# Weight conversions on VectorE and paced by step, the third pair of a Strassen-Winograd MLP in round one from its fifth chunk on, sums in PSUM, and mixing tiles in the tokens' places

## Chip, core and metric

One core of a Trainium2 chip runs the whole kernel. The metric is device microseconds of one execution. PE is TensorE, DVE is VectorE, ACT is ScalarE, POOL is GpSimd, and SP is the engine that issues all loads and stores here. All large products are made of three float32r products (high x high, high x low, low x high), so every operand stands as a high part and a low part (the rest that rounding leaves).

## The reference

Sizes: batch 8, 8 heads, 576 tokens, 512 channels, 2048 hidden channels; all weights arrive as float64.

```python
def phi(x):
    proj = np.einsum('bhsd,df->bhsf', x, w_phi)
    proj = proj - np.max(np.abs(proj), axis=-1, keepdims=True)
    return np.concatenate([np.exp(proj), np.exp(-proj)], axis=-1)
# attention: linear attention with phi(q), phi(k); num / den
# MLP: layer norm over 512 channels, then
    ch = np.maximum(xn @ w_ch1, 0.0) @ w_ch2
    x = x + ch
# mixing:
    theta = x @ w_theta
    y = (np.einsum('ts,bsd->btd', w_tok_r, x * cos(theta))
         + np.einsum('ts,bsd->btd', w_tok_i, x * sin(theta)))
    u = x + y
    out = u + np.maximum(u @ w_ch, 0.0)
```

## The kernel before

The time has four parts. **Attention** takes the first 600 us or so. The layer norm and the first quarter of the MLP (`mlp_a`, four of sixteen blocks of 128 hidden channels) run beside it in 18 chunks of 256 tokens and go on for its last six chunks after it; `tokens` in `mlp_a` transposes the normalised tokens on PE, ACT takes the high part from PSUM, DVE the low part, and the sum of both goes to DRAM as `xnd` for later.

**Pair rounds.** The other twelve hidden blocks are six pairs. A `Pair` holds the seven combinations of two 256 x 256 weight blocks that a Strassen-Winograd product needs (`wa`) and its part of the second weight (`wd`). Tokens go in nine chunks of 512; `tokens_b` loads a chunk (`xt`), forms four sums or differences, and splits seven operands (a11, a12, a22, s1 to s4) into high (ACT) and low (DVE). Round one runs pairs 0 to 2 over the nine chunks, round two pairs 3 to 5; a step is one pair on one chunk. In a step `Hidden.first` and `second` make the seven products in PSUM (tiles pa, of which there are two, pb and pc, one each), DVE adds what belongs together, ACT makes the relu's high part and DVE its low part. `flush_b` makes the down part of the step before (24 matmuls of 512 columns into four accumulators `acc`). Between rounds the sum of residual and output goes through DRAM (`xqd`).

**Conversion.** A float64 weight block comes in as 64-bit integers (`raw`, three places). ACT takes the magnitude, DVE makes three instructions of integer bits and one product (L110, L111, L112, L117), ACT writes the high part. Low parts (`lo_pool`, L66) and the four weight differences `tw` (L587 to L590) of the pairs are on POOL. A pair is six pieces of such work (`prep` yields six times). One piece is asked for after each step, at low priority; the scheduler that orders the instructions on each engine may place it earlier. Pairs 0 to 2 are converted before round one, pairs 3 to 5 in it, and the mixing's weights (26 pieces, `loads_mix`) in round two.

**Mixing.** For each batch: transposes of the tokens (`tp`), theta (`th`), its sine and cosine through ACT, DVE and POOL, the product over tokens (`mx`), and the channel product (`ch`).

Each engine works off its instructions in a fixed order, which the scheduler writes at build time. SP's queue is in order too.

## Time and profile before

| | us |
|---|---|
| three timed runs | 1777.98, 1778.2, 1774.35 (median 1777.98) |
| profiled execution | 1779.11, of which the span from first to last instruction is 1777.3 |
| PE busy | 1677.1 (94%) |
| DVE busy | 1286.8 (72%) |
| ACT busy | 805.4 (45%) |
| POOL busy | 781.8 (44%) |

The page counts an engine as busy from an instruction's start to its end; neighbouring instructions overlap a little, so a sum of durations is larger than the busy time. PE's granted clock is 1.00 where it runs at its upper level (2.4 GHz); a mean below that says that a part of a stretch ran at the lower one (1.2 GHz).

### The profile page before, as it was taken

To read this page: it belongs to the slowest core of one execution; us is meant where nothing else is said; L and a number is where in the kernel's file an instruction comes from. 1 tells how busy PE (TensorE), PEld (TensorE's weight loads), DVE (VectorE), ACT (ScalarE), POOL (GpSimd) and SP (SyncE) were. 2 spreads that over 40 slices of the span, in tenths; PEclk is the share of its full clock that TensorE was granted. 3 is DMA by queue.
4 is the path that set the end of the run, shared out by engine and by line. 5 is a ranking of instruction groups with operands and counts; after the bars stand their busy time and mean duration, and the time that the engine had idled before them with its cause. 6 is when DMAs were issued, how large, how long until landed. Compare 5 with 4: busy or idle time off the path is not lost.

```text
span 1777.3 us, 29747 instructions
## 1 busy us (share of the span) xinstructions
PE 1677.1 (94%) x11272; PEld 1524.4 (86%) x11272; DVE 1286.8 (72%) x2292; ACT 805.4 (45%) x1644; POOL 781.8 (44%) x684
## 2 busy tenths in 40 slices
PE   7899999899999888879999998999989999999999
PEld 5787998898899687768988887888978999999999
DVE  8988898888887696995555699555547656656662
ACT  6675666566666444543333354333333223322230
POOL 7786787687685376651111333121123222222220
PEclk9999999999999999999999999999999999999999
DMA  5333333233331454653231676331271211112101
GB/s 192 86 106 117 97 108 111 78 110 117 103 119 48 140 177 169 236 167 108 96 118 72 252 244 228 101 143 72 88 251 37 69 51 38 55 46 67 59 20 41
DMA packets 107966, 201.65 MB, mean 113 GB/s; under 512 B 8368, under 2 KB 58416, under 8 KB 104496
## 3 DMA queue, kind: packets, MB, share of 16 engines
q1 hardware_dynamic: 107824, 199.76, 34.1%
q8 instruction: 89, 1.46, 0.4%
q14 instruction: 53, 0.43, 0.1%
HBM read 125.73 MB, written 69.80 MB: 110 GB/s over the span
## 4 chain that ended last, share of the span: by engine, by line
PE 67%; DVE 20%; issue 4%; POOL 4%; ACT 3%; DMA 2%; SPq 0%; DVEq 0%; POOLq 0%; ACTq 0%
PE acc L77 5%; PE acc L75 5%; PE acc L76 5%; PE mx L75 4%; PE mx L76 4%; PE mx L77 4%; PE pa L76 2%; PE pa L77 2%; PE pa L75 2%; DVE bits L111 2%; PE ch L77 2%; PE ch L75 2%; PE ch L76 2%; DVE bits L112 2%; DVE hl L703 2%
## 5 line engine op out<-in xcount | busy, mean ns | idle before, releaser
L75 PE MATMUL acc<-wd,hh 128*128 128x512 f32 x432 | 173.5, 402 | 7.2 <-ACT hh L702 4.2
L77 PE MATMUL acc<-wd,hl 128*128 128x512 f32 x432 | 163.7, 401 | 16.2 <-DVE hl L703 16.2
L76 PE MATMUL acc<-wd,hh 128*128 128x512 f32 x432 | 172.6, 400 | 0.0
L633 POOL TENSOR_TENSOR s<-xt 128x512 f32<-128x512 f32 x18 | 26.3, 1462 | 310.4 <-DMA xt<-xnd 283.2
L75 PE MATMUL mx<-xs 128*128 128x288 f32 x512 | 151.1, 296 | 0.5 <-POOL xs L57 0.4
L76 PE MATMUL mx<-xs 128*128 128x288 f32 x512 | 151.2, 296 | 0.0
L77 PE MATMUL mx<-xs 128*128 128x288 f32 x512 | 149.4, 296 | 0.0
L273 DVE TENSOR_TENSOR ys<-pj,m 128x512 f32<-128x512 f32 (+1 forms) x160 | 99.6, 626 | 34.0 <-ACT pf L283 19.3
L703 DVE SCALAR_TENSOR_TENSOR hl<-c,hh 128x256 fp32r<-128x256 f32 x162 | 101.1, 630 | 22.6 <-ACT hh L702 22.4
L77 PEld LDWEIGHTS acc<-wd,hl 128*128 128x128 f32 x432 | 80.1, 189 | 38.9 <-DVE hl L703 22.1
L271 DVE TENSOR_REDUCE m<-pj 128x4 f32<-128x512 f32 (+1 forms) x160 | 98.6, 622 | 13.7 <-PE pj L77 13.1
L57 POOL TENSOR_SCALAR xs<-sc 128x512 fp32r<-128x512 f32 x72 | 47.5, 659 | 134.8 <-DVE sc L935 133.2
L702 ACT ACTIVATE hh<-c 128x256 fp32r<-128x256 f32 x162 | 66.4, 415 | 85.0 <-DVE c L696 82.7
L66 POOL TENSOR_TENSOR kpl<-pf,kph 128x512 fp32r<-128x512 f32 (+1 forms) x75 | 96.2, 1283 | 19.4 <-ACT kph L60 16.8
L75 PEld LDWEIGHTS acc<-wd,hh 128*128 128x128 f32 x432 | 82.9, 192 | 21.3 <-ACT hh L702 5.2
L283 ACT ACTIVATE pf<-ys 128x512 f32<-128x512 f32 (+1 forms) x160 | 85.5, 586 | 34.0 <-DVE ys L273 13.3
L66 POOL TENSOR_TENSOR qp<-pf,qp 128x512 fp32r<-128x512 f32 (+1 forms) x66 | 80.6, 1226 | 39.8 <-ACT qp L60 39.6
L75 PEld LDWEIGHTS mx<-xs 128*128 128x128 f32 x512 | 96.2, 188 | 1.4 <-POOL xs L57 1.2
L696 DVE TENSOR_TENSOR c<-pc,u 128x256 f32<-128x256 f32 x108 | 44.9, 416 | 71.9 <-ACT u L691 71.7
L76 PEld LDWEIGHTS mx<-xs 128*128 128x128 f32 x512 | 96.2, 188 | 0.0
L77 PEld LDWEIGHTS mx<-xs 128*128 128x128 f32 x512 | 95.6, 188 | 0.1
L76 PE MATMUL kv<-kpl,vh 128*65 128x256 f32 x300 | 87.9, 293 | 6.2 <-DVE kpl L63 6.0
(263 smaller groups left out, 6157.1 us busy)
## 6 DMA issues: line engine op xcount, KB each, us to landing
xt<-xnd SPq DMA_DIRECT2D x36, 512.0 KB, 4.7
raw<-in_w SPq DMA_DIRECT2D x32, 512.0 KB, 4.2
in<-in_va SPq DMA_DIRECT2D x30, 325.0 KB, 3.0
xd<-xo SPq DMA_DIRECT2D x48, 192.0 KB, 2.1
x<-xd SPq DMA_DIRECT2D x36, 256.0 KB, 2.9
xnd<-xt SPq DMA_DIRECT2D x18, 512.0 KB, 3.4
xpd<-x SPq DMA_DIRECT2D x36, 256.0 KB, 2.2
x<-xpd SPq DMA_DIRECT2D x18, 512.0 KB, 4.5
```

Of the source, the lines that this page charges most:

```text
L57: G.tensor_scalar(dst, src, scale, 0.0, op0=ALU.mult, op1=ALU.add)
L66: G.tensor_tensor(dst, src, f32(hi), op=ALU.subtract)
L75: T.matmul(out_, lhsT=lh, rhs=rh, start=start, stop=False, **kw)
L76: T.matmul(out_, lhsT=lh, rhs=rl, start=False, stop=False, **kw)
L77: T.matmul(out_, lhsT=ll, rhs=rh, start=False, stop=stop, **kw)
L111: V.scalar_tensor_tensor(bits, hi32, -(1 << 30), bits, op0=ALU.bitwise_and, op1=ALU.bitwise_or)
L271: V.tensor_reduce(m[:, :2 * n], pv, axis=AX.X, op=ALU.max, apply_absolute_value=True)
L273: V.tensor_tensor(ys[:, :2 * n, :], pv, m[:, :2 * n].unsqueeze(2).to_broadcast([P, 2 * n, NF]), op=ALU.subtract)
L283: A.activation(kp[:, :2 * n, s, :], ys[:, :2 * n, :], AF.Exp, scale=sc)
L696: V.tensor_tensor(c, ps, t, op=ALU.add)
L702: A.activation(h, c, AF.Relu)
L703: V.scalar_tensor_tensor(l, c, 0.0, f32(h), op0=ALU.max, op1=ALU.subtract)
```

## The change

Low parts and weight differences of the conversions go from POOL to DVE. Only pairs 0 and 1 are converted before round one; pair 2 is converted during the first four chunks, which have two steps each, and takes part from the fifth chunk on. Round two makes up for it: its first four chunks have four steps (pairs 2 to 5). `advance` sets how many pieces have been asked for after each step: 24 over the 22 steps of round one, and the 26 of the mixing from the fifth chunk of round two on. The first chunk's token sums are on DVE. The copy of the transposed tokens for DRAM, in chunks after the attention, is an ACT copy from PSUM in place of a POOL sum. DVE's sums for c11 and c12 are written back into pb and pc; c22 uses a place of `raw` until the conversions are over. The mixing's tiles take the places of the token tiles, its weights are loaded during the last chunk, and its first tiles are prepared ahead of the last down part.

```diff
@@ tokens, in mlp_a
-                G.tensor_tensor(xt[:, :, o], f32(xh[:, :, o]), f32(xl[:, :, o]), op=ALU.add)
+                if wide(ch):
+                    A.activation(xt[:, :, o], tp, AF.Copy)
+                else:
+                    G.tensor_tensor(xt[:, :, o], f32(xh[:, :, o]), f32(xl[:, :, o]), op=ALU.add)
@@ Pair.prep
-            G.tensor_tensor(t[:, 0], b12, b11, op=ALU.subtract)
+            V.tensor_tensor(t[:, 0], b12, b11, op=ALU.subtract)
...
-                lo(dl, x, dh)
+                lo_vec(dl, x, dh)
...
-    spare = Pair(NR + 1, NR)
-    slots = [Pair(m, m) for m in range(NR)]
-    gl = (None for q in slots for _ in q.prep(p_st))
+    early = [Pair(m, m) for m in range(2)]
+    gl = (None for q in early for _ in q.prep(p_st))
@@ tokens_b
-        G.tensor_tensor(s1, a21, a22, op=ALU.add)
-        G.tensor_tensor(s2, s1, a11, op=ALU.subtract)
-        G.tensor_tensor(s3, a11, a21, op=ALU.subtract)
-        G.tensor_tensor(s4, a12, s2, op=ALU.subtract)
+        eng.tensor_tensor(s1, a21, a22, op=ALU.add)
+        eng.tensor_tensor(s2, s1, a11, op=ALU.subtract)
...
+            if n == "s1":
+                eng.tensor_tensor(s3, a11, a21, op=ALU.subtract)
+                eng.tensor_tensor(s4, a12, s2, op=ALU.subtract)
...
-    cur = tokens_b(0)
+    cur = tokens_b(0, V)
@@ loads_mix (three places)
-            split64(p_st, wth[:, c, :], wths[c][:, 0, :], wths[c][:, 1, :], pool_lo=True)
+            split64(p_st, wth[:, c, :], wths[c][:, 0, :], wths[c][:, 1, :])
@@ Hidden
-            c11 = self.plus(b, p1, "c11")
-            self.relu(c11, 0, 0)
+            V.tensor_tensor(b, b, p1, op=ALU.add)
+            self.relu(b, 0, 0)
...
-            c22 = self.plus(c, u3, "c22")
-            self.relu(c22, 1, 1)
+            t = p_st.tile([P, NC_], F32, name="c22", tag="raw", bufs=RAWB) if pace else p_hb.tile([P, NC_], F32, name="c22")
+            V.tensor_tensor(t, c, u3, op=ALU.add)
+            self.relu(t, 1, 1)
...
-            c12 = self.plus(self.c, self.u2, "c12")
-            self.relu(c12, 0, 1)
+            V.tensor_tensor(self.c, self.c, self.u2, op=ALU.add)
+            self.relu(self.c, 0, 1)
@@ loads_b
+        prs[2] = Pair(2, 2)
+        yield from prs[2].prep(p_st)
+        for i in range(2):
+            q = Pair(4 + i, 3)
             yield from q.prep(p_st)
+            q.keep(wx_d[i])
+        prs[3] = Pair(3, 3)
+        yield from prs[3].prep(p_st)
@@ the rounds
+    LOADB, LOADX = 24, 26
+    def advance(r, to):
+        goal = (LOADB, LOADX)[r] * to
+        with tc.high_priority(offset=LOWP):
+            while steps[r] < goal:
+                next(gl if r == 0 else gx, None)
+                steps[r] += 1
...
+            ms = ([0, 1] + ([2] if ch >= LATE else [])) if r == 0 else (([2] if ch < LATE else []) + [3, 4, 5])
...
+                if r == 0:
+                    if ch < LATE:
+                        advance(0, done / (2 * LATE) * 6 / LOADB)
+                    else:
+                        advance(0, 6 / LOADB + (done - 2 * LATE) / (3 * (NQ - LATE) - 2) * (1 - 6 / LOADB))
+                elif ch >= LATE:
+                    advance(1, min(1, (done - 4 * LATE) / (3 * (NQ - LATE) - 4)))
@@ the mixing's start
     x4, pre = shared_prep(0)
     bs[0].start(x4)
+    early(0)
     shared(0, pre)
+    early(1)
+    bs[0].theta(0)
+    flush_b()
@@
+LATE = 4
```

Three places show how the engines' orders move. POOL in round one, from the token sums of its second chunk on (`s` is a token sum, `tw`, `wa` and `wd` are the pair's conversion); before:

```order
L633 TENSOR_TENSOR s_9675<-xt 128x512
L635 TENSOR_TENSOR s_9677<-xt 128x512
L634 TENSOR_TENSOR s_9676<-s_9675,xt 128x512
L636 TENSOR_TENSOR s_9678<-xt,s_9676 128x512
L587 TENSOR_TENSOR tw<-vs 128x256
L588 TENSOR_TENSOR tw<-vs 128x256
L589 TENSOR_TENSOR tw<-vs,tw 128x256
L66 TENSOR_TENSOR wa_8264<-vs,wa_8264 128x512
```

and now (the token sums are named `c`):

```order
L647 TENSOR_TENSOR c_9502<-xt 128x512
L652 TENSOR_TENSOR c_9504<-xt 128x512
L648 TENSOR_TENSOR c_9503<-c_9502,xt 128x512
L653 TENSOR_TENSOR c_9505<-xt,c_9503 128x512
L647 TENSOR_TENSOR c_9750<-xt 128x512
L652 TENSOR_TENSOR c_9752<-xt 128x512
```

Between one chunk's token sums and the next one's POOL has nothing left. DVE in round one, from a c11 sum on (of the fifth step before, `c<-pb`, and of the fourth now, `pb<-pb`); before:

```order
L696 TENSOR_TENSOR c_9846<-pb,p_9838 128x256
L110 TENSOR_SCALAR bits<-raw 128x512
L111 SCALAR_TENSOR_TENSOR bits<-raw,bits 128x512
L746 TENSOR_TENSOR x<-acc_9394,x 128x512
L696 TENSOR_TENSOR c_9769<-pc,u_9767 128x256
L746 TENSOR_TENSOR x<-acc_9395,x 128x512
L112 SCALAR_TENSOR_TENSOR bits<-raw,bits 128x512
L703 SCALAR_TENSOR_TENSOR hl<-c_9846,hh 128x256
L703 SCALAR_TENSOR_TENSOR hl<-c_9769,hh 128x256
L703 SCALAR_TENSOR_TENSOR hl<-pa,hh 128x256
L117 SCALAR_TENSOR_TENSOR val<-mag,bits 128x512
```

and now:

```order
L720 TENSOR_TENSOR pb<-pb,p_9669 128x256
L63 TENSOR_TENSOR wa<-vs,wa 128x512
L594 TENSOR_TENSOR tw<-vs,tw 128x256
L63 TENSOR_TENSOR wa<-vs,wa 128x256
L63 TENSOR_TENSOR a11l<-xt,a11h 128x512
L756 TENSOR_TENSOR xo<-acc_9328,xo 128x512
L756 TENSOR_TENSOR xo<-acc_9329,xo 128x512
L63 TENSOR_TENSOR a12l<-xt,a12h 128x512
L728 TENSOR_TENSOR c_9597<-pc,u_9595 128x256
L63 TENSOR_TENSOR wa<-tw,wa 128x512
L712 SCALAR_TENSOR_TENSOR hb<-pb,hb 128x256
```

The low parts of `wa` now stand in DVE's queue between the sums and the relus; the steps after this one hold no conversion. PE at the first transpose of the mixing (`tp`), inside the last down part (`acc`); before:

```order
L77 MATMUL acc_15405<-wd_12477,hl 128x512
L910 MATMUL tp<-ident,x 128x128 x4
L75 MATMUL acc_15402<-wd_12477,hh 128x512
L76 MATMUL acc_15402<-wd_12477,hh 128x512
L75 MATMUL acc_15403<-wd_12477,hh 128x512
L76 MATMUL acc_15403<-wd_12477,hh 128x512
L77 MATMUL acc_15402<-wd_12477,hl 128x512
L77 MATMUL acc_15403<-wd_12477,hl 128x512
L75 MATMUL th<-xs,xh 128x512
```

and now:

```order
L937 MATMUL tp<-ident,xs 128x128 x4
L77 MATMUL acc_15280<-wd,hb 128x512
L77 MATMUL acc_15281<-wd,hb 128x512
L75 MATMUL acc_15280<-wd,hb 128x512
L76 MATMUL acc_15280<-wd,hb 128x512
L77 MATMUL acc_15280<-wd,hb 128x512
L75 MATMUL acc_15281<-wd,hb 128x512
L76 MATMUL acc_15281<-wd,hb 128x512
L77 MATMUL acc_15281<-wd,hb 128x512
L75 MATMUL acc_15278<-wd,hb 128x512
L76 MATMUL acc_15278<-wd,hb 128x512
```

The transposes moved ahead by eight matmuls of the down part; four more of these follow the rows shown.

## Rows read from the trace of the kernel before

**Rows 1.** The page: busy time, share of the span and instructions of each engine.

```profile
span 1777.3 us, 29747 instructions
...
PE 1677.1 (94%) x11272; PEld 1524.4 (86%) x11272; DVE 1286.8 (72%) x2292; ACT 805.4 (45%) x1644; POOL 781.8 (44%) x684
```

**Rows 2.** Busy time by stretch: length, PE, weight loads, DVE, ACT, POOL, clock, DMA.

```profile
100.00:150.00 50.00, 49.66 (x379) 43.19 (x378) 43.77 (x94) 35.59 (x71) 39.25 (x34) 1.00 0.40 114
597.00:690.60 93.60, 83.04 (x496) 73.16 (x494) 80.15 (x123) 35.73 (x69) 57.23 (x42) 0.93 0.52 173
690.60:797.00 106.40, 84.56 (x474) 72.42 (x475) 97.79 (x136) 51.19 (x116) 61.40 (x46) 0.94 0.59 208
797.00:1000.00 203.00, 202.77 (x1262) 181.73 (x1261) 112.00 (x208) 74.62 (x180) 32.91 (x25) 1.00 0.34 121
1000.00:1110.00 110.00, 99.68 (x588) 86.50 (x586) 104.36 (x187) 53.53 (x131) 46.22 (x37) 0.97 0.68 229
1110.00:1174.00 64.00, 62.58 (x386) 55.58 (x387) 37.36 (x65) 23.14 (x57) 12.87 (x9) 1.00 0.35 120
1312.00:1360.00 48.00, 40.41 (x211) 32.73 (x210) 37.25 (x55) 21.12 (x36) 23.13 (x27) 0.96 0.34 106
```

**Rows 3.** Waits of PE from 690.6 to 797: us in total, times, longest.

```profile
PE acc L77 <- DVE hl L703: 11.2, 6, 3.2
```

**Rows 4.** DVE by groups, 690.6 to 797: busy us, mean ns, idle before.

```profile
L111 DVE SCALAR_TENSOR_TENSOR bits<-raw,bits 128x512 int32<-128x512 int32 x14 | 17.5, 1247 | 0.3
L703 DVE SCALAR_TENSOR_TENSOR hl<-c,hh 128x256 fp32r<-128x256 f32 x21 | 14.9, 721 | 1.0 <-ACT hh L702 1.0
L112 DVE SCALAR_TENSOR_TENSOR bits<-raw,bits 128x512 int32<-128x512 int32 x13 | 11.7, 901 | 0.1
L110 DVE TENSOR_SCALAR bits<-raw 128x512 int32<-128x512 int32 x14 | 11.3, 807 | 0.1
L117 DVE SCALAR_TENSOR_TENSOR val<-mag,bits 128x512 f32<-128x512 f32 x13 | 10.7, 823 | 0.1
...
L703 DVE SCALAR_TENSOR_TENSOR hl<-pa,hh 128x256 fp32r<-128x256 f32 x7 | 2.9, 411 | 0.0
```

**Rows 5.** DVE by groups, 797 to 1000.

```profile
L112 DVE SCALAR_TENSOR_TENSOR bits<-raw,bits 128x512 int32<-128x512 int32 x2 | 1.4, 685 | 0.0
L111 DVE SCALAR_TENSOR_TENSOR bits<-raw,bits 128x512 int32<-128x512 int32 x1 | 0.7, 693 | 0.0
L110 DVE TENSOR_SCALAR bits<-raw 128x512 int32<-128x512 int32 x1 | 0.4, 426 | 0.0
```

**Rows 6.** Timeline of DVE, 848 to 850.2: start, us.

```profile
848.41 0.68 DVE L63 TENSOR_TENSOR a22l<-xt,a22h 128x512 fp32r<-128x512 f32 x1
849.01 0.69 DVE L63 TENSOR_TENSOR s4l<-s,s4h 128x512 fp32r<-128x512 f32 x1
```

**Rows 7.** Timeline of DVE, 855 to 859.

```profile
855.96 1.37 DVE L703 SCALAR_TENSOR_TENSOR hl<-c,hh 128x256 fp32r<-128x256 f32 x1
857.25 0.41 DVE L696 TENSOR_TENSOR c<-pb,p 128x256 f32<-128x256 f32 x1
857.59 0.41 DVE L703 SCALAR_TENSOR_TENSOR hl<-pa,hh 128x256 fp32r<-128x256 f32 x1
```

**Rows 8.** Timeline of POOL, 855 to 859.

```profile
855.74 1.31 POOL L635 TENSOR_TENSOR s<-xt 128x512 f32<-128x512 f32 x1
857.00 1.48 POOL L634 TENSOR_TENSOR s<-s,xt 128x512 f32<-128x512 f32 x1
```

**Rows 9.** Waits of PE from 1312 to 1360.

```profile
PE th L75 <- ACT xh L60: 3.1, 3, 1.6
PE tp L910 <- DMA x<-x2d: 2.9, 1, 2.9
```

**Rows 10.** The page's DMA issues: KB each, median us from issue to landing.

```profile
xt<-xnd SPq DMA_DIRECT2D x36, 512.0 KB, 4.7
raw<-in_w SPq DMA_DIRECT2D x32, 512.0 KB, 4.2
```

More of the change, by code (lines that the diff above doesn't have):

```diff
@@ L731, in down @@
                     o = slice(i * P, (i + 1) * P)
[L732 to L733 removed]
+                    mm3(acc[i], self.hb[:, 0, j, o], self.hb[:, 1, j, o], self.q.wd[:, 0, j, :],
+                        self.q.wd[:, 1, j, :], start and j == 0, stop and j == 1)
     def flush_b():
[L736 to L739 removed]
+        hid, acc, r, ch, first, last = pend
+        hid.down(acc, first, last)
+        if last:
+            x = p_hb.tile([P, 2 * CT, DM], F32, name="xo")
             if r == 0:
@@ L819, in body @@
-    wtks = [t[:, i] for q in slots for t in [in_slot("wa", q.slot, [3, 2, S])] for i in range(3)]
-    wtk_t = wtks
-    wchs = [t[:, i] for q in slots[:2] for t in [in_slot("wd", q.slot, [2, 2, DM])] for i in range(2)]
-    wths = [(t[:, 0, :], t[:, 1, :]) for t in wths]
-    wtks = [(t[:, 0, :], t[:, 1, :]) for t in wtks]
+                pend = (hid, acc, r, ch, n == 0, n == len(ms) - 1)
+                if n == len(ms) - 1 and not (r and last):
+                    cur = tokens_b(0 if last else ch + 1, G)
@@ new lines, in body @@
+                done += 1
+                if r == 0:
[5 more added lines that the diff above has]
+                    advance(1, min(1, (done - 4 * LATE) / (3 * (NQ - LATE) - 4)))
+                if r and last:
+                    k = (3, 0, 1)[n]
+                    t = in_slot("wa", k, [3, 2, S])
+                    for i in range(3):
+                        wtks[MIXO[3 * n + i]] = t[:, i]
+                        SY.dma_start(out=f32(t[:, i]), in_=wtk_d[MIXO[3 * n + i]])
@@ L824, in body @@
+                if r == 0 and last and n >= 1:
+                    prs[3 + n] = Pair(3 + n, n - 1).back(wx_d[n - 1])
+            if r and ch == NQ - 2:
+                advance(1, 1)
+                s_st.close()
+                pace = False
+        if r == 0:
+            advance(0, 1)
+    s_ps.close()
     s_xm, pm = opened(name="xm", bufs=1, side="left")
+    s_ps = ExitStack()
+    ps_tr, ps_th = pool("xtp", 1), pool("xth", 2)
     class Slots:
@@ L1001, in body @@
     s_ps.close()
-    s_p1.close()
+    s_ac.close()
     s_xm.close()
-    s_xc.close()
+    s_hb.close()
+    s_xb.close()
     s_wb.close()
```

183 lines of the change are left out of this document (82 added, 101 removed).

## The prediction

> **What bounds the kernel now.** I read the page's shares first: PE is busy 94% of a span of 1777.3 us [rows 1]. The change alters no matmul: the order of the built programs holds 11174 PE instructions on both sides. So it can only give back time in which PE stands or runs slowly. The second view, busy time by stretch, shows where that is [rows 2]. From 797 to 1000 us PE is full: 1262 matmuls in 203 us, 6.217 per us, so a step of the pair rounds (66 matmuls by the code: 42 of the up part, 24 of the down part) takes 10.62 us. At that pace the 474 matmuls of 690.6 to 797 are 76 us of work in 106 us: 30 lost. The 588 of 1000 to 1110 are 94.6 in 110: 15 lost; 1110 to 1174 loses 2 more. Before round one (597 to 690.6) shapes differ, so I count idle time, 93.6 - 83.0 = 10.6, and the lower clock, 7% of 83 = 5.8: 16 lost. The start of the mixing (1312 to 1360) loses 7.6 + 4% of 40 = 9 likewise. In all 72 us; a change of this kind can't give back more.
>
> In the three stretches that hold conversions DVE is busy 86%, 92% and 95%; from 797 to 1000, where it is 55%, nothing is lost [rows 2]. The list of waits says whom PE waits for in round one: the down part for the low halves of the relu on DVE, 11.2 us in six waits [rows 3]. The groups of DVE say why these come late [rows 4, 5]: in the conversion stretch the first or of the bits (L111) takes 1247 ns against 693 in the quiet stretch, the shift (L110) 807 against 426, and the relu that reads its sum from SBUF (L703, hl<-c) 721, while the same relu that reads PSUM (hl<-pa) stays at 411. The timeline shows the partner: a relu of 1.37 us [rows 7] lies on POOL's subtraction of 1.31 us that began at 855.74 [rows 8]. So POOL, busy 57 to 61 us in each of the first two stretches, lengthens the DVE instructions that read two tiles of SBUF, and those stand in one queue with the relus.
>
> The Trainium skill states this as a rule ("SBUF — State Buffer", section Who interferes with whom): a DVE instruction with two SBUF inputs and a GpSimd instruction that reads SBUF block each other for a whole instruction, one with a single SBUF input doesn't. The trace agrees (1.37 against 0.41 us).
>
> **The change, part by part.** *Conversions to DVE alone.* One 512-column instruction after another costs DVE 0.60 us (848.41 to 849.01) [rows 6], one of 256 columns 0.34 (857.25 to 857.59) [rows 7], a shift 0.35 (0.426 [rows 5] less the same overlap of 0.08). What moves from POOL is 38 differences of 512 columns, 18 of 288 (0.39 by the ratio of columns and a little), 30 of 256, and the first chunk's four sums: 22.8 + 7 + 10.2 + 2.4 = 42 us more on DVE. What it takes off, in 690.6 to 797: L111 14 x (1247 - 693) = 7.8; L112 13 x (901 - 685) = 2.8; L110 14 x (807 - 426) = 5.3; L117 13 x (823 - 685) = 1.8; relu 21 x (721 - 411) = 6.5 [rows 4, 5]: 24 us, and an estimated 6 on the low halves of the tokens: 30, or 0.49 per us of POOL. Four sets of token sums, each sum about 1.4 us [rows 8], are 22 of POOL's 61 us there and stay; 39 x 0.49 = 19 goes. In the stretch before, POOL is left with nearly nothing; at two thirds of that ratio, since more of DVE's work there reads PSUM, 57 x 0.33 = 19 goes. From 1000 to 1110 three sets of sums (17 of 46 us) stay and 29 x 0.49 = 14 goes. Together 52 off, 42 on: DVE's total falls by only some 10 us.
>
> *Pacing decides, then.* **Before round one** two pairs are converted, not three: eight blocks of weights pass DVE there, twelve before. DVE's 80 us [rows 2] become 80 - 19 - 4 x 2.15 (one shift, three of 0.60) + 12 (moved work of two pairs, token sums) = 64, beside some 77 us of PE (93.6 less the 16 lost). The twelve token copies go to ACT, which is busy 36 of 93.6 us [rows 2]; at about 0.6 us each they take 7 of its free 58, the next tile's high half behind them. If that cover were gone, 7. The waits at the end of the attention stay. I leave 6 of the 16: **10 back**.
>
> **Round one** has its conversions over 22 steps (234 us) instead of about 8. DVE there: 16 blocks x 2.15 = 34; moved work of four pairs 19; seven own instructions a step, 22 x 2.4 = 53; 8.5 sets of seven token halves at 0.60, 36; output sums 8 x 2.4 = 19: 161 us, and 12 to 25 for what POOL's token sums still lengthen (nine sets, 50 us of POOL, at 0.49 or, since two in three of the SBUF relus will now read PSUM, half of it). That is 74 to 79% of 234. A row for the lower end is 100 to 150 us, in the attention: DVE 88% busy, PE idle 0.34 of 50 [rows 2], 0.7%, 2 us here. The upper end is the line between 55% (nothing) and 92% (30 of 106): at 76%, 16%, 37 us, more than is lost now. I take 4%, 9 us, near the lower end, because the long instructions that a relu finds ahead of it fall from 1.2 us to 0.7. **21 back.**
>
> **The mixing's weights** come in 12 steps (127 us) instead of about 9.5: 18 blocks of 288 columns at 1.4 + 0.39, 8 of 512 at 2.75, 12 x 2.4 own, four chunks at 4.2 + 2.4: 54 + 29 + 26 = 109, and 10 of lengthening: 119, 94%. Ends: 0.7% and the 14% that 95% cost (15 of 110); I take 7%, 9 of 127, against 17: **8 back**.
>
> **Start of the mixing.** The first transposes stand before 14 matmuls of the last down part, not 6, 3.3 us of cover instead of 1.4 (a step's 10.62 us over 42 + 2 x 24 units of 256 columns is 0.118 us a unit). PE's waits for the copies of a transpose (3.1) and a load (2.9) [rows 9] shrink; the chain from theta to the first mix stays, since its instructions do. Between 0 and 6: **4 back**.
>
> **Sums in PSUM.** The add costs the same (hl<-pa and c<-pb at 0.41 [rows 7]), its result is read without POOL's lengthening (part of the 24 above). PE's bank is held until the relu has read it: behind that stands the next pair's product in the same bank, 16 down and 12 up matmuls later (5.2 us) by the order; the chain add, relu on ACT, relu on DVE is about 2 us. At nothing, then. **Two steps a chunk** in the first four chunks: the load of the tokens (4.7 us [rows 10]), POOL's four sums behind it (1.4 each) and the halves must then fit into 21 us instead of 32, behind the same SP queue. They fit, with less room; I charge 2 us, and 16 are possible, some 4 (a load's time) at each of four borders.
>
> Sum: 10 + 21 + 8 + 4 - 2 = 41 back on 1779.11 us, the profiled execution's own time, 1.13 over the median of the three runs: 1738, or 1737 as a median. The good ends, with all 16 of the first stretch, give back 66; the poor ends lose 10 or so.
>
> **Rivals.** (a) *DVE stays the bound.* The Trainium skill says ("Perfetto Trace Analysis", section Optimizing Scalar/DVE Operations) that work of a saturated DVE may be offloaded to ScalarE or even GpSimd, and that the shared port may spoil it; by its first half this change goes the wrong way. By rows: 42 us arrive on an engine that is 92 to 95% busy where it matters, and round one keeps its loss by the straight line, the mixing's weights too: 10 + 0 + 0 + 4 - 2 = 12 back, 1766. For it: DVE's sum falls by 10 only; against it: 88% busy cost 0.7% in the attention. (b) *Tokens and rings come late*: c22 takes its place in the ring of three raw tiles, so loads of 4.2 us [rows 10] can start later (4 to 12 us of DVE work between release and use by the order, 5 to 13 before), and two-step chunks wait for their tokens: 16 to 20 us dearer, 1755. (c) *No change*: the losses come from the queue's order, not from its length, and move with the conversions: 1776 to 1781. (d) *Slower*: the bank of pc. The chain that frees it is 2 us and may have two or three conversions of 0.6 in it, 3.8 us; PE comes back after 5.2. If DVE is late by 3 us in every step, PE waits 1.6 x 54 = 86 less the 41: 1823. It decides against the change from 0.8 us of waiting per step, a chain of 6.0 us.
>
> **Numbers.** Chances: forecast 0.63, (a) 0.17, (b) 0.11, (c) 0.05, (d) 0.04. Under 0.2% (3.6 us) this kernel's runs can't tell a change: their spread is 3.9. Faster takes the forecast, (a) and (b): 0.91; same 0.05; slower 0.04. The forecast's own range is 1720 to 1753; for 8 in 10 I take 1714 (all terms at their good ends give 1713) to 1764, which holds (b) and a part of (a).
>
> **What would show it.** L111 and L110 at about 0.70 and 0.43 us outside POOL's four token sums; relus on pb and pc at 0.41; POOL almost idle from 600 to 690; the first pair matmul at about 680 rather than 690.6; round one without a wait over 2 us for hb; DVE 75 to 80% busy in it and 90% or more while the mixing's weights come. I am wrong if PE waits for pc or pb products at each step, for tokens at the borders of the first four chunks, or if DVE's rows stay long with POOL idle.

## The result, and the profile after

The changed kernel takes 1737.28 us (median of four runs, 1736.38 to 1738.16); the kernel before took 1777.92 beside it. The ratio is 0.9776, 95% interval 0.9759 to 0.9793: faster, by 40.6 us, where 41 were predicted. The profiled execution took 1738.16 us, against 1779.11 before.

The sum is right, but not all of its terms are: the rounds gave 5.3 us more than predicted and the last stage 5.4 less. Three stages can be compared exactly, because they begin and end at the same matmul in both kernels. In the predicted column round one, the mixing's weights and the two-step chunks are one figure (21 + 8 - 2).

| stage | before | after | back | predicted |
|---|---|---|---|---|
| start to the first pair matmul (`pa`) | 690.6 | 680.6 | 10.0 | 10 |
| from there to the end of the last down matmul (`acc`) | 623.6 | 591.3 | 32.3 | 27 |
| from there to the end of the span | 463.1 | 464.5 | -1.4 | 4 |

Busy time by stretch of the changed kernel (length, PE, weight loads, DVE, ACT, POOL, clock, DMA) answers to [rows 2]: the end of the attention, the 22 steps of round one, a quiet stretch, the mixing's weights, the start of the mixing.

```profile
587.00:680.60 93.60, 86.06 (x545) 75.85 (x544) 63.78 (x142) 40.68 (x77) 2.24 (x2) 0.96 0.46 155
680.60:915.00 234.40, 225.88 (x1389) 201.68 (x1388) 184.06 (x349) 111.16 (x266) 48.05 (x34) 0.99 0.49 174
915.00:1104.00 189.00, 189.00 (x1186) 170.77 (x1185) 86.81 (x178) 63.21 (x161) 24.24 (x19) 1.00 0.29 106
1104.00:1250.00 146.00, 141.87 (x873) 125.55 (x872) 131.03 (x274) 70.57 (x176) 22.60 (x16) 1.00 0.65 219
1268.00:1317.00 49.00, 37.07 (x188) 30.74 (x186) 36.13 (x52) 20.84 (x33) 23.15 (x26) 0.90 0.36 116
```

The reader is to see four things. POOL is almost idle before round one, and DVE has 63.8 us of work there (64 predicted). In round one PE is idle for 8.5 of 234 us, where before it was idle for 21.8 of the first 106 alone; DVE is 79% busy, the upper of the two figures predicted. While the mixing's weights come DVE is 90% busy and PE idles 4 us of 146, and the quiet stretch ahead of it loses nothing. The start of the mixing alone has become no better: 37 of 49 us, at a clock of 0.90.

PE's waits in the 22 steps of round one (us in total, times, longest) answer to [rows 3], where one group alone had 11.2:

```profile
PE pc L76 <- DVE s1l L63: 2.5, 1, 2.5
PE pa L75 <- ACT u L705: 1.9, 1, 1.9
PE acc L77 <- DVE hb L712: 1.7, 3, 0.7
PE acc L75 <- ACT hb L711: 1.0, 1, 1.0
```

DVE's groups there (busy us, mean ns, idle before) answer to [rows 4]; L712 is now the relu's low half.

```profile
L712 DVE SCALAR_TENSOR_TENSOR hb<-c,hb 128x256 fp32r<-128x256 f32 x21 | 13.2, 628 | 0.6 <-ACT hb L711 0.5
L111 DVE SCALAR_TENSOR_TENSOR bits<-raw,bits 128x512 int32<-128x512 int32 x15 | 12.0, 803 | 0.3
L110 DVE TENSOR_SCALAR bits<-raw 128x512 int32<-128x512 int32 x16 | 9.4, 590 | 1.0 <-DMA raw<-in_w 0.9
L712 DVE SCALAR_TENSOR_TENSOR hb<-pb,hb 128x256 fp32r<-128x256 f32 x22 | 9.1, 415 | 0.5 <-ACT hb L711 0.5
L712 DVE SCALAR_TENSOR_TENSOR hb<-pc,hb 128x256 fp32r<-128x256 f32 x20 | 8.3, 416 | 1.9 <-ACT hb L711 1.8
```

The or of the bits (L111) has fallen from 1247 to 803 ns, and the relus on PSUM stand at 415. Only the sum that stays in SBUF (`c`, c22) keeps a relu of 628 ns. The means of L111 hide two kinds: by the timeline 13 of the 15 take 0.68 to 0.70 us with no POOL instruction beside them, and the two that a token sum on POOL overlaps take 1.44 and 1.67.

To divide the second stage, and for the experiments, I use one more measure, the **loss**: for each matmul the time from its start to the start of the next one, less the usual distance for its shape (0.119 us for 256 columns; else the median in the same run), summed. It counts idle time and lower clock together. "Round one" is its first 22 steps, "round two" the other 32 pair steps up to the last down part. Kernels whose round one has the same code differ by up to 2 us in it (13.5 to 15.6 below).

| loss, us | round one | round two |
|---|---|---|
| before | 32.8 | 18.3 |
| after | 14.8 | 6.8 |

So 18 came back in round one (predicted 21 - 2) and 11.5 in round two (predicted 8). The other 2.8 of the 32.3 us lie nearly all in the usual distance itself: for the 1296 down matmuls of 512 columns it is 0.231 us in the changed kernel and 0.233 in the kernel before. No run shows why.

By the same measure, step by step, 6 to 9 us of round one's loss stand in its first two steps in every kernel below but e2 (13.6 there). In steps 3 to 22 the kernel before loses 24.3 us and the changed one 6.1; kernels of the same code there lie between 6.1 and 7.2.

### The profile page after: what moved, and what is told of

It is laid out like the page before. It is cut to its first block, busy times and chain, and to the rows that moved or that the text cites. A ratio compares the mean times of both kernels' runs of the same rounds, so it can differ in the third digit from the quotient of the medians.

```text
span 1736.4 us, 29670 instructions
## 1 busy us (share of the span) xinstructions
PE 1660.0 (96%) x11272; PEld 1516.9 (87%) x11272; DVE 1254.6 (72%) x2382; ACT 806.5 (46%) x1656; POOL 653.7 (38%) x582
## 4 chain that ended last, share of the span: by engine, by line
PE 70%; DVE 16%; POOL 4%; issue 4%; DMA 3%; ACT 3%; SPq 0%; DVEq 0%; POOLq 0%; ACTq 0%
PE acc L77 5%; PE acc L75 5%; PE acc L76 5%; PE mx L75 4%; PE mx L76 4%; PE mx L77 4%; PE pa L75 2%; PE pa L77 2%; PE pa L76 2%; PE ch L77 2%; PE ch L76 2%; PE ch L75 2%; PE th L77 2%; PE th L76 2%; PE th L75 2%
## 5 line engine op out<-in xcount | busy, mean ns | idle before, releaser
L647 POOL TENSOR_TENSOR c<-xt 128x512 f32<-128x512 f32 x17 | 22.7, 1338 | 531.2 <-DMA xt<-xnd 320.9
L75 PE MATMUL mx<-xs 128*128 128x288 f32 x576 | 172.1, 300 | 10.1 <-POOL xs L57 10.1
L75 PE MATMUL acc<-wd,hb 128*128 128x512 f32 x432 | 171.1, 396 | 2.7 <-ACT hb L711 1.7
L76 PE MATMUL acc<-wd,hb 128*128 128x512 f32 x432 | 170.8, 395 | 0.0
L76 PE MATMUL mx<-xs 128*128 128x288 f32 x576 | 170.0, 296 | 0.0
L77 PE MATMUL mx<-xs 128*128 128x288 f32 x576 | 168.3, 296 | 0.2 <-DVE xs L63 0.2
L77 PE MATMUL acc<-wd,hb 128*128 128x512 f32 x432 | 154.3, 395 | 3.7 <-DVE hb L712 3.7
L75 PEld LDWEIGHTS mx<-xs 128*128 128x128 f32 x576 | 108.8, 189 | 11.4 <-POOL xs L57 11.3
L76 PEld LDWEIGHTS mx<-xs 128*128 128x128 f32 x576 | 108.9, 189 | 0.0
L272 DVE TENSOR_REDUCE m<-pj 128x4 f32<-128x512 f32 (+1 forms) x160 | 98.6, 622 | 13.7 <-PE pj L77 12.9
L77 PEld LDWEIGHTS mx<-xs 128*128 128x128 f32 x576 | 107.9, 188 | 0.5 <-DVE xs L63 0.5
L57 POOL TENSOR_SCALAR xs<-xs 128x512 fp32r<-128x512 f32 x72 | 48.4, 673 | 133.1 <-DVE xs L962 131.5
L75 PEld LDWEIGHTS acc<-wd,hb 128*128 128x128 f32 x432 | 82.1, 190 | 17.0 <-ACT hb L711 3.4
L76 PEld LDWEIGHTS acc<-wd,hb 128*128 128x128 f32 x432 | 82.1, 190 | 11.9
L77 PEld LDWEIGHTS acc<-wd,hb 128*128 128x128 f32 x432 | 76.8, 190 | 17.6 <-DVE hb L712 6.0
L63 DVE TENSOR_TENSOR kpl<-pf,kph 128x512 fp32r<-128x512 f32 (+2 forms) x75 | 87.8, 1171 | 5.1 <-ACT kph L60 4.4
L60 ACT ACTIVATE u<-xT 128x288 fp32r<-128x288 f32 x64 | 28.1, 440 | 134.7 <-DVE xT L911 125.5
```

The lines of the kernel that those rows point to most:

```text
L57: G.tensor_scalar(dst, src, scale, 0.0, op0=ALU.mult, op1=ALU.add)
L60: A.activation(dst, src, AF.Copy)
L63: V.tensor_tensor(dst, src, f32(hi), op=ALU.subtract)
L75: T.matmul(out_, lhsT=lh, rhs=rh, start=start, stop=False, **kw)
L76: T.matmul(out_, lhsT=lh, rhs=rl, start=False, stop=False, **kw)
L77: T.matmul(out_, lhsT=ll, rhs=rh, start=False, stop=stop, **kw)
```

## The experiments

The prediction had two reasons for the 27 us of the rounds: DVE's instructions get short because POOL is gone, and the conversions are spread over more steps, which the change puts down to `advance`. Theory T says that both are needed. The rivals are each alone, and a theory R that came from the order of the built programs: `c22`, which takes a place in the ring of three raw tiles at every step, holds the conversions back, not the counts of `advance`. The stage columns below are those of the first table; times are medians, with the ratio to the kernel before in the same comparison.

| kernel | us | ratio, 95% interval | to first `pa` | rounds | to the end | loss, round one | loss, round two |
|---|---|---|---|---|---|---|---|
| before | 1777.92 | | 690.6 | 623.6 | 463.1 | 32.8 | 18.3 |
| after | 1737.28 | 0.9776 [0.9759, 0.9793] | 680.6 | 591.3 | 464.5 | 14.8 | 6.8 |
| e1: conversions' POOL work back | 1754.13 | 0.986 [0.9834, 0.9886] | 685.2 | 602.8 | 464.5 | 12.9 | 20.2 |
| e2: before, that work on DVE | 1751.76 | 0.9844 [0.9817, 0.987] | 686.7 | 603.1 | 463.1 | 21.9 | 8.7 |
| e3: c22 outside the ring | 1743.97 | 0.9798 [0.9773, 0.9823] | 680.3 | 597.7 | 464.2 | 24.5 | 3.5 |
| e4: c11, c12 in SBUF | 1746.53 | 0.9817 [0.9781, 0.9853] | 678.7 | 600.5 | 464.2 | 17.7 | 13.1 |
| e5: first theta ahead | 1737.81 | 0.9774 [0.9757, 0.979] | 678.8 | 592.1 | 466.5 | 15.6 | 6.8 |
| e6: mixing's weights over all of round two | 1731.37 | 0.9741 [0.9725, 0.9758] | 679.0 | 585.0 | 465.5 | 13.6 | 1.6 |
| e7: mixing's start on ACT | 1737.16 | 0.9761 [0.9746, 0.9776] | 681.4 | 591.7 | 464.7 | 14.8 | 7.2 |
| e8: e1 and e6 together | 1738.37 | 0.9766 [0.9751, 0.9781] | 685.0 | 586.2 | 465.0 | 13.5 | 3.0 |
| e9: tokens for DRAM back on POOL | 1736.01 | 0.9755 [0.9742, 0.9769] | 679.1 | 590.2 | 465.0 | 13.5 | 7.0 |
| e10: e6 and e7 together | 1731.55 | 0.9731 [0.9718, 0.9745] | 678.2 | 587.1 | 464.3 | 14.4 | 3.0 |
| e11: e4 and e6 together | 1738.79 | 0.9781 [0.9764, 0.9799] | 678.9 | 589.7 | 465.5 | 15.5 | 4.5 |
| e12: before, c22 in the ring | 1765.87 | 0.993 [0.9914, 0.9947] | 688.5 | 596.9 | 477.4 | 11.0 | 13.8 |

**e1, the move undone.**

```diff
-            V.tensor_tensor(t[:, 0], b12, b11, op=ALU.subtract)
+            G.tensor_tensor(t[:, 0], b12, b11, op=ALU.subtract)
...
-                lo_vec(l[:, d], x, h[:, d])
+                lo_pool(l[:, d], x, h[:, d])
...
-            split64(p_st, wth[:, c, :], wths[c][:, 0, :], wths[c][:, 1, :])
+            split64(p_st, wth[:, c, :], wths[c][:, 0, :], wths[c][:, 1, :], pool_lo=True)
```

> Undoes one part of the change: the low parts and the weight differences of all conversions go back to POOL; order by step, third pair and all else stay. Theory T (both parts are needed: the spreading gives DVE room, and POOL's absence keeps its instructions short): POOL lengthens DVE's two-input instructions again, the bits' first or (L111) is at about 1.0 us or more instead of 0.70, PE waits again for the down part's low halves, and 8 to 20 of the 41 us are lost: 1745 to 1757. Rival P (the spreading alone gives the 41): within 3 us of the changed kernel, 1734 to 1741, although DVE's rows are long again. Rival M (the move alone gives them): close to the kernel before, 1770 or more.

17 us were lost, in T's range, but not where it said; and as 24 of the 41 us are left, the move isn't needed for all of the gain. Busy time of e1 in three parts of the rounds:

```profile
685.20:917.50 232.30, 224.29 (x1388) 200.28 (x1387) 170.54 (x309) 111.99 (x266) 91.04 (x74) 0.99 0.49 175
917.50:1107.00 189.50, 189.50 (x1190) 171.34 (x1189) 84.87 (x178) 63.22 (x160) 23.75 (x18) 1.00 0.29 106
1107.00:1265.00 158.00, 145.61 (x863) 127.72 (x862) 131.84 (x247) 69.34 (x174) 50.38 (x42) 0.97 0.58 199
```

DVE's L111 in the first of them:

```profile
L111 DVE SCALAR_TENSOR_TENSOR bits<-raw,bits 128x512 int32<-128x512 int32 x15 | 14.8, 985 | 0.3
```

In round one POOL works 91 us instead of 48 and L111 takes 985 ns instead of 803, and PE loses no more by it: 12.9 us of loss against 14.8. So in round one the spreading alone gives what both give. Of the 16.1 us by which the profiled spans differ, 4.6 lie before round one and 11.5 in the rounds: 13.4 of loss more in round two, where the mixing's weights come, and 1.9 less in round one. There PE idles 12.4 of 158 us, although DVE is only 83% busy, less than the 90% of the changed kernel. The longest of these waits, at 1170 us, shows one way in which it happens. The timeline of ACT (start, length; in brackets idle time before and what ended it):

```profile
1165.15 0.61 ACT L60 ACTIVATE s2h<-c 128x512 fp32r<-128x512 f32 x1
1169.83 0.46 ACT L109 ACTIVATE mag<-raw 128x288 f32<-128x288 f32 x1 [4.06 <-DMA raw<-in_wtok]
1170.19 0.36 ACT L711 ACTIVATE hb<-pa 128x256 fp32r<-128x256 f32 x1
```

PE in the same place:

```profile
1170.61 0.80 PE L75 MATMUL acc<-wd,hb 128*128 128x512 f32 x1 [3.87 <-ACT hb L711]
```

SP's queue ahead of it:

```profile
1159.11 6.55 SPq L682 DMA_DIRECT2D wtkd<-wc  x3
1165.76 1.83 SPq L103 DMA_DIRECT2D raw<-in_wtok  x2
```

and the list of SP's waits from 1107 to 1265:

```profile
SPq L682 <- POOL wc L66: 41.4, 17, 6.1
```

The store of a finished weight (L682) waits in SP's queue for POOL's low part (41.4 us in 17 waits). Behind it stands the next load of raw weights, which goes out at 1165.76. ACT waits 4.06 us for it with the relu behind, and PE 3.87 us for that relu. The step that holds this wait (the 45th, from 1161.2 to 1180.4) loses 8.7 of round two's 20.2 us. This is rival (b)'s kind of cost, late loads, here behind a store that waits for POOL. The queue's wait alone doesn't make the loss: in the changed kernel the same store waits for DVE (33.0 us in 18 waits from 1104 to 1250), and in e8 below it waits for POOL for 86.6 us in 14 waits, with hardly any loss.

**e2, the move alone.** The same edits, made in the kernel before.

```diff
-        def prep(self, stage, lo=lo_pool):
+        def prep(self, stage, lo=lo_vec):
...
-            G.tensor_tensor(t[:, 0], b12, b11, op=ALU.subtract)
+            V.tensor_tensor(t[:, 0], b12, b11, op=ALU.subtract)
...
-            split64(p_st, wth[:, c, :], wths[c][:, 0, :], wths[c][:, 1, :], pool_lo=True)
+            split64(p_st, wth[:, c, :], wths[c][:, 0, :], wths[c][:, 1, :])
```

> Does one part alone: the kernel before, with nothing but its low parts and weight differences moved from POOL to DVE. The order still bunches the conversions (nine steps at the start of round one, ten in round two; up to 16.8 us of undisturbed DVE work fall on one step of 10.6). Theory T: DVE's rows become short, yet its sum stays above PE's in the bunched steps, so round one and the mixing's weights keep most of their loss; the tail before round one gains some: 1760 to 1772. Rival M (the move alone does it): 1737 to 1745. Rival (a) of the prediction (DVE is the bound, more work on it hurts): 1778 or more.

It gave 27 us, which lies between T's range and M's. By the profile 3.9 came before round one, 20.5 in the rounds (10.9 of loss in round one, 9.6 in round two). In steps 3 to 22 the loss falls from 24.3 to 8.3 us; its first two steps lose 5 more than those of the kernel before. So the move pays also where the work stays bunched (L110, the shift that each converted block needs, stands in steps 1 to 8 in the trace of e2, in 2 to 8 before), and rival (a) falls: some 40 us of work more on an engine that was 92 to 95% busy there made the kernel faster, and DVE's busy time in all fell from 1286.8 to 1272.6 us. In the bunched stretch there is still a loss, with DVE busy 103 of 113 us:

```profile
686.70:800.00 113.30, 102.85 (x584) 90.38 (x585) 102.84 (x185) 58.89 (x133) 24.41 (x16) 0.91 0.58 206
```

**e3, c22 outside the ring.**

```diff
-            t = p_st.tile([P, NC_], F32, name="c22", tag="raw", bufs=RAWB) if pace else p_hb.tile([P, NC_], F32, name="c22")
+            t = p_hb.tile([P, NC_], F32, name="c22")
```

> The changed kernel, with c22 in a tile of its own instead of a place of the ring of three raw tiles; the numbers in advance stay. By the order the pairs' conversions then bunch in the first 12 steps of round one (up to 15.7 us of DVE work in a step) and the mixing's in steps 36 to 45. Theory R (the ring, not advance, is what spreads the work): 8 to 20 us lost, 1745 to 1757, with PE waiting for low halves from 690 to 810 and from 1060 to 1170. Rival (b) of the prediction (the ring's share for c22 only makes loads late): same or up to 5 us faster, 1732 to 1738. Rival A (advance spreads): same within 2 us.

6.7 us were lost in all, a little less than R's lower end, but round one behaved as R said: 9.7 us of loss more, with `advance` unchanged.

```profile
680.30:800.00 119.70, 106.85 (x636) 92.95 (x635) 114.42 (x208) 64.15 (x147) 31.51 (x20) 0.97 0.68 239
```

DVE is 96% busy in it: by the trace L110 stands in steps 2 to 13, where the changed kernel has it in steps 2 to 22 (none in 4 to 6). All of the loss lies in steps 1 to 11. In the other eleven, with c22 in the same tile of its own, there is none, so it isn't the tile itself that costs.

In round two R was wrong: the loss fell by 3.3, and not by spreading. L110 of the mixing's weights stands in nine steps here (37 to 45) and in eleven in the changed kernel (41 to 51). From 1085 to 1180 DVE is 96% busy, and PE still works for 92.9 of the 95 us. Busy time of the stretch that holds all of these steps:

```profile
1060.00:1200.00 140.00, 137.89 (x857) 123.27 (x856) 117.16 (x254) 66.84 (x168) 21.90 (x16) 1.00 0.57 193
```

So a place in the ring for c22 may cost something there, as rival (b) had it; no run tells it apart from the other order.

**e12, the ring alone.** One edit to the kernel before.

```diff
-            c22 = self.plus(c, u3, "c22")
+            c22 = p_st.tile([P, NC_], F32, name="c22", tag="raw", bufs=RAWB)
+            V.tensor_tensor(c22, c, u3, op=ALU.add)
```

> The kernel before with one edit: c22 takes a place of the ring of three raw tiles. Low parts and differences stay on POOL, three pairs are converted before round one, a piece is asked for after each step, as before. By the order the ring alone spreads the pairs' blocks over steps 1 to 18 (before: about nine) and the mixing's over steps 28 to 53. Theory R (the ring spreads, and spreading is what the rounds gain by): 14 to 20 us back in round one, 10 to 16 in round two, nothing before round one, and up to 10 lost at the start of the mixing, whose last weights now come late: 1745 to 1758. Rival (b) of the prediction (in the ring the loads come late): 1778 or more. Rival (DVE needs the move too): 1765 to 1775.

26.7 us came back in the rounds, 21.8 of loss in round one. That is more than the whole change gave in round one, with POOL's work, three pairs before it and one piece a step as before. By the trace L110 now stands in steps 2 to 19, and steps 3 to 22 lose 2.6 us. Busy time of e12 in about the stretch of [rows 2] that lost most:

```profile
688.50:797.00 108.50, 103.23 (x627) 91.30 (x627) 76.21 (x129) 50.64 (x117) 42.96 (x34) 0.97 0.42 147
```

DVE's L111 in its round one:

```profile
L111 DVE SCALAR_TENSOR_TENSOR bits<-raw,bits 128x512 int32<-128x512 int32 x12 | 8.2, 686 | 0.2
```

627 matmuls, where [rows 2] have 474 in 106.4 us. And L111 is at 686 ns although the low parts are on POOL: by the timeline none of the twelve falls beside a POOL instruction. The run as a whole gained only 12.6 us. That is the last rival's range (1765 to 1775), not R's, but the stages say that it is not for the rival's reason: round one gave more than R asked, round two 4.5 instead of 10 to 16, and the stage after the last down matmul costs 14.3 us more than before. There SP still stores and loads weights when the rounds end, and the loads of the mixing's first tokens (L908) go out behind them:

```profile
1280.25 0.32 SPq L672 DMA_DIRECT2D wcd<-wc  x1
...
1287.14 2.14 SPq L908 DMA_DIRECT2D x<-x2d  x3
```

PE's longest wait follows from it:

```profile
1293.75 1.12 PE L911 MATMUL tp<-ident,x 128*128 128x128 f32 x4 [8.38 <-DMA x<-x2d]
```

R holds for round one; its figures for the rest were wrong.

**e6, the mixing's weights over all of round two.**

```diff
-        for c in range(KC):
-            split64(p_st, wth[:, c, :], wths[c][:, 0, :], wths[c][:, 1, :])
-            yield
...
+        for c in range(KC):
+            split64(p_st, wth[:, c, :], wths[c][:, 0, :], wths[c][:, 1, :])
+            yield
...
-                elif ch >= LATE:
-                    advance(1, min(1, (done - 4 * LATE) / (3 * (NQ - LATE) - 4)))
+                else:
+                    advance(1, min(1, done / (4 * LATE + 3 * (NQ - LATE) - 4)))
```

> The changed kernel, with the mixing's weights spread over all of round two (token weights first, theta's last) instead of from its fifth chunk on; by the order one piece stands in each step from 24 to 49, with at most 10.2 us of undisturbed DVE work in a step. Theory S (what is left of the loss from 1104 to 1250, 7 us, is DVE at 90 per cent): 4 to 7 us faster, 1730 to 1734, DVE at 75 to 80 per cent in both halves of the round. Rival (the left-over is the chunk borders and POOL's token sums, not the pieces): within 2 us of the changed kernel.

S holds: 1731.37 us (1730.47 to 1733.26, no overlap with the changed kernel's runs), 5.2 us of loss gone, and from 1104 to 1250 PE is busy for 144.5 of 146 us with DVE at 67% (65% from 912 to 1104), where 75 to 80 were forecast:

```profile
912.00:1104.00 192.00, 192.00 (x1204) 173.45 (x1203) 125.47 (x263) 77.03 (x197) 25.60 (x19) 1.00 0.44 152
1104.00:1250.00 146.00, 144.50 (x905) 130.19 (x904) 98.46 (x194) 58.94 (x143) 21.33 (x16) 1.00 0.50 174
```

The edit also puts theta's weights last, which isn't told apart from the spreading. This version beats both kernels.

**e8, spread, with POOL.** The edits of e1 and e6 together.

```diff
-                lo_vec(l[:, d], x, h[:, d])
+                lo_pool(l[:, d], x, h[:, d])
...
-                elif ch >= LATE:
-                    advance(1, min(1, (done - 4 * LATE) / (3 * (NQ - LATE) - 4)))
+                else:
+                    advance(1, min(1, done / (4 * LATE + 3 * (NQ - LATE) - 4)))
```

> The kernel with the low parts and differences back on POOL lost nothing in round one (22 steps for 24 pieces) and 13 us while the mixing's weights came (12 steps for 26 pieces). Here the same kernel has these 26 pieces spread over all of round two. Theory P2 (lengthening by POOL costs only where DVE has no room; with the work spread thin it costs nothing): 10 to 15 us are regained, 1739 to 1744, and what stays behind the changed kernel with spread pieces is the tail before round one, 5 us. Theory L (POOL's lengthening costs in itself): at least 8 us lost from 915 us to the last down matmul, 1747 or more.

P2 holds, at 0.6 us below its range: 15.8 of e1's 17 us were regained, and the rounds take 586.2 us, 1.2 more than in e6. What remains is 6.0 us before round one. In round one POOL is busy 90 us and L111 still at 985 ns; in the two parts of round two PE idles 0.4 and 1.8 us, with POOL at work for 39 and 34:

```profile
685.00:918.00 233.00, 226.35 (x1389) 201.81 (x1388) 171.12 (x310) 111.90 (x265) 89.75 (x73) 0.99 0.49 175
918.00:1107.00 189.00, 188.58 (x1181) 170.09 (x1180) 114.58 (x239) 74.17 (x190) 38.65 (x35) 1.00 0.44 154
1107.00:1265.00 158.00, 156.25 (x971) 140.30 (x970) 99.14 (x196) 63.76 (x154) 33.95 (x27) 1.00 0.50 177
```

The rule of the Trainium skill ("SBUF — State Buffer", section Who interferes with whom), that a DVE instruction with two SBUF inputs contends with a GpSimd instruction that reads SBUF, is seen here too: L111 takes 985 ns against 803 in the changed kernel. It decides nothing: here, where the engine has room, its instructions are longer at hardly any cost.

**e4 and e11, the sums in SBUF**, in the changed kernel and in e6. The two sums share one place, since there was no room for two.

```diff
-            V.tensor_tensor(b, b, p1, op=ALU.add)
-            self.relu(b, 0, 0)
+            c11 = p_hb.tile([P, NC_], F32, name="c11", tag="cs")
+            V.tensor_tensor(c11, b, p1, op=ALU.add)
+            self.relu(c11, 0, 0)
...
-            V.tensor_tensor(self.c, self.c, self.u2, op=ALU.add)
-            self.relu(self.c, 0, 1)
+            c12 = p_hb.tile([P, NC_], F32, name="c12", tag="cs")
+            V.tensor_tensor(c12, self.c, self.u2, op=ALU.add)
+            self.relu(c12, 0, 1)
```

> The changed kernel, with the sums c11 and c12 in tiles of SBUF instead of being written back to PSUM. The prediction costed this edit at nothing but for a part of the lengthening by POOL's token sums (nine sets in round one, 50 us of POOL, 0.49 against half of that: 12 us of DVE in 234, where DVE is 79 per cent busy). Theory: 0 to 4 us slower, 1737 to 1741, the relus on these sums at 0.5 to 0.7 us on the mean instead of 0.41. Rival (d) of the prediction (holding the bank costs PE): faster by 2 us or more, because the bank comes free sooner.

> Sums c11 and c12 in SBUF cost the changed kernel 9 us, 3 of them in round one and 6 while the mixing's weights came in 12 steps. Here the same edit is made where those weights are spread over all of round two (1731.4 with the sums in PSUM). Theory V (the sums cost because DVE had no room there: longer relus and an order that heaps up to 14 us of undisturbed DVE work on a step): the 6 us vanish, 1732 to 1736. Rival (the sums in SBUF cost in themselves, by POOL or by a later bank): again 7 to 11 us, 1738 to 1742.

Both theories were too low. e4 is 9.2 us slower than the changed kernel. e11 is 7.4 us slower than e6, in the rival's range, so by the medians room on DVE takes away little of the cost. By the profiled executions it takes away half: the edit adds 9.2 us to the rounds in e4 (6.3 of loss in round two) and 4.7 in e11 (2.9). e11's is the fastest of its four runs, and the runs of e4 lie 8.5 us apart. So V is neither borne out nor refuted. New in e4 are PE's waits for the sum of c12, which are not in the changed kernel's list; here from 1104 to 1250:

```profile
PE acc L75 <- ACT hb L711: 4.6, 4, 2.1
PE pc L75 <- DVE c L737: 3.1, 3, 1.8
```

Whether the longer relus, the place that both sums share or the other order on DVE costs this stays open.

**e9, the tokens for DRAM back on POOL.**

```diff
-                if wide(ch):
-                    A.activation(xt[:, :, o], tp, AF.Copy)
-                else:
-                    G.tensor_tensor(xt[:, :, o], f32(xh[:, :, o]), f32(xl[:, :, o]), op=ALU.add)
+                G.tensor_tensor(xt[:, :, o], f32(xh[:, :, o]), f32(xl[:, :, o]), op=ALU.add)
```

> The changed kernel, with the copies of the transposed tokens for DRAM back on POOL in the chunks after the attention (twelve sums of 512 columns, some 20 us of POOL between 600 and 680). The prediction's tail before round one rests on POOL's absence and on fewer weight blocks on DVE. Theory C (POOL beside a DVE that reads two tiles lengthens it): 2 to 5 us of the 10 are lost, the first pair matmul at 682.5 to 685.5, run 1739 to 1742. Rival (DVE has room there now, 64 us of work in 94): within 1.5 us of the changed kernel.

The rival holds: 1736.01 us and a first pair matmul at 679.1, with POOL busy 19.9 us before it instead of 2.2. The copies on ACT gave nothing.

**e5, e7 and e10, the start of the mixing.** e5 puts the first theta ahead of the shared one; e7 copies batch 0's tokens on ACT and loads the sine's table early; e10 is e7 on top of e6.

```diff
-    shared(0, pre)
-    early(1)
     bs[0].theta(0)
+    early(1)
+    shared(0, pre)
```

> The changed kernel, with the second early transposes and batch 0's first theta emitted ahead of the shared preparation at the start of the mixing. In the changed kernel three thetas stand back to back from 1271.7 to 1280.9 and PE then idles 8.7 us for the cosine and sine of the first of them. Theory Z (the chain behind the first theta on ACT, POOL and DVE sets the first mix): the first mix comes 2 to 5 us earlier after the last down matmul, 1732 to 1736. Rival (the engines work that chain off at their pace whichever comes first): within 1.5 us of the changed kernel.

```diff
+            if self.b == 0:
+                A.activation(o, self.pre[i][3], AF.Copy)
+            else:
+                G.tensor_tensor(o, f32(self.pre[i][1]), f32(self.pre[i][2]), op=ALU.add)
...
+    A.activation(pm.tile([P, 1], F32, name="sin0"), halfpi, AF.Sin)
     x4, pre = shared_prep(0)
```

> The changed kernel, with two edits at the start of the mixing: batch 0's transposed tokens are copied by ACT from PSUM instead of summed by POOL from SBUF, and ACT's table for the sine is loaded by a one-element sine ahead of the mixing instead of at the first theta (1.28 us at 1278.95 in the changed kernel, inside the chain to the first mix). Theory Z (the chain from the first thetas through ACT, DVE and POOL sets the start): without the load (1.28) and POOL's lengthening of DVE's rows there (1.40 instead of 0.41, 1.09 instead of 0.68) the first mix comes 3 us earlier after the last down matmul, and the run is 2 to 4 us faster: 1733 to 1735.5. Rival Y (what the first mix gains is waited for at the next ones, as where the first theta was put ahead): within 1.5 us of the changed kernel.

> The mixing's weights spread over all of round two, which was 6 us faster than the changed kernel (1731.4), with the two edits at the start of the mixing (ACT's copies for batch 0, the sine's table loaded ahead). Theory Z: 2 to 4 us faster again, 1727.5 to 1729.5. Rival Y: 1730 to 1732.5.

In e5 the first mix came 15.5 us after the last down matmul, in e7 15.9, against 17.9 in the changed kernel. Neither run became faster (1737.81 and 1737.16), and e10 equals e6. In e7 the one long wait for the first mix is 5.5 instead of 8.7 us, but the thetas ahead of it wait more (3.5 instead of 1.6), so the list of PE's waits shrinks by little:

```profile
PE mx L75 <- POOL xs L57: 7.0, 3, 5.5
PE th L75 <- ACT xs L60: 3.5, 4, 1.3
```

Rival Y holds: two us gained at the first mix are gone at the end. What sets the length of this start was not found.

## Why the prediction came out right, and where it did not

The forecast of 41 us was met within 0.4, and that is luck in part: 5.3 us too few in the rounds and 5.4 too many at the start of the mixing cancel. Two of its signs came out well: without a POOL instruction beside them L111 takes 687 ns and L110 421 in the changed kernel's round one (0.70 and 0.43 forecast). But DVE's total was to fall by some 10 us and fell by 32 (1286.8 to 1254.6): 14.2 by the move alone (e2), 19.5 by the ring alone (e12). And it gives 11174 PE instructions, where the profile counts 11272 on both sides; that the change adds none holds.

**Before round one: right.** 10 us and 680, measured 10.0 and 680.6, with DVE's work as forecast. e1 and e8, which have POOL's conversions but only two pairs there, reach 685: about half of the 10 comes from the third pair being gone and half from the move; the move alone gave 3.9 (e2). The cover for the token copies on ACT held, and the copies were worth nothing (e9).

**Round one: right size, wrong cause.** The heading "pacing decides, then" was right, but the prediction took the 22 steps from the change, which names `advance` for them, and didn't ask what holds a piece back. One piece a step had been asked for before as well. What stops the scheduler from placing pieces earlier is the ring, which each step's c22 passes through in turn: without it round one loses 9.7 of the 18 us again (e3), and the ring alone gives 21.8 (e12). In the prediction c22 in the ring stood as rival (b)'s cost. The chain of the prediction from POOL to lengthened rows to late relus is real: where the work stays bunched, taking POOL away gives 10.9 (e2). Where the work is spread it costs next to nothing: e1 and e8 have the long L111 and lose no more in round one than the changed kernel. The move and the spreading are two cures for one fault, so their gains don't add: 10.9 (e2), 19.9 (e1), 18.0 together.

One reading behind this chain was too narrow. The prediction says that POOL lengthens the instructions that read two tiles of SBUF, and that by the Trainium skill one with a single SBUF input isn't blocked. Its own row of L110, which reads one tile, says otherwise (807 against 426 ns), and in the changed kernel L110 takes 0.42 us alone and up to 1.5 beside a token sum on POOL. The Trainium skill excepts the 2-port perf modes there, which the prediction left out; whether L110 runs in one, no run shows.

**The mixing's weights: mis-sized.** 8 back was the term; 11.5 came back, from a loss of 18.3 and not 17. I took 7% of 127 us as remaining loss (9); it was 6.8, and DVE was 90% busy, not 94%. The straight line from DVE's share to PE's loss, the upper bound there, is not a law: 90% cost 7 us of 146 in the changed kernel, 83% cost about 20 of 158 in e1, where a load came late as well, and 96% cost 2 of 95 in e3. Here the move counts: undoing it costs 13.4 us in 12 steps, and nearly nothing in 26 (e8).

**Start of the mixing: wrong.** The term was 4 back; 1.4 were lost. The step that failed is that PE's waits for the transposes would turn into time. The first theta starts 0.16 us before the last down matmul ends in both kernels, whether the transposes stand before 6 or 14 of its matmuls. PE in the kernel before, then in the changed one:

```profile
1313.60 0.63 PE L77 MATMUL acc<-wd,hl 128*128 128x512 f32 x2
1314.07 0.39 PE L75 MATMUL th<-xs,xh 128*128 128x512 f32 x1
...
1330.87 0.60 PE L75 MATMUL mx<-xs,czh 128*128 128x288 f32 x1
```

```profile
1271.27 0.62 PE L77 MATMUL acc<-wd,hb 128*128 128x512 f32 x2
1271.72 0.39 PE L75 MATMUL th<-xs 128*128 128x512 f32 x1
...
1280.63 0.39 PE L77 MATMUL th<-xs 128*128 128x512 f32 x1
1289.76 0.61 PE L75 MATMUL mx<-xs 128*128 128x288 f32 x1 [8.75 <-POOL xs L57]
1290.17 0.45 PE L76 MATMUL mx<-xs 128*128 128x288 f32 x1
1290.41 0.45 PE L75 MATMUL mx<-xs 128*128 128x288 f32 x1
...
1293.61 0.30 PE L76 MATMUL mx<-xs 128*128 128x288 f32 x1
...
1294.41 0.30 PE L75 MATMUL mx<-xs 128*128 128x288 f32 x1
1294.54 0.29 PE L76 MATMUL mx<-xs 128*128 128x288 f32 x1
```

The short waits of [rows 9] did shrink (1.6 for the copy, none for the load). PE then ran three thetas back to back and stood 8.75 us for the chain behind them, where before it had stood in pieces; the first mix came 16.6 us after the last down matmul before and 17.9 now, which is nearly all of the 1.4.

**Sums in PSUM, two-step chunks.** "At nothing" holds for the bank: PE's list has no wait for it that recurs, and rival (d) did not come. But undoing the edit costs 7 to 9 us by the medians, which the prediction did not see. Behind the first step no wait for tokens shows in the list; the 2 us charged can't be told from the rest, since no run changes the two-step chunks alone.

**Rivals.** (a) is refuted by e2; (c) was the nearest to the truth about the queue's order, and wrong that the loss would move along with the conversions. (b) did not happen as forecast; the 3.3 us that round two gains in e3 are the most that may be its. (d) did not happen.

## What to carry to other kernels

Ask first what holds a background task back, and don't take the place where the code asks for it for the place where it runs: a buffer that it shares with the main loop can be the true pace, and one line that shares it gave back two thirds of round one's loss (and cost 14.3 us at the next stage, whose loads came late). Find out how much of a step each engine has to spare before counting contention: the same work on POOL cost 13 us in 12 steps and about 1 in 26. And follow a wait to the end of its chain before booking its removal: a wait of the first engine that is only ahead of a longer one is worth nothing.
